# Attention with normalised q and k, followed by an MLP, on one core: order of the first loads, a held reduction, and transposes in another PSUM bank

## The chip, the core and the metric

The kernel runs on one core of a Trainium2 chip. A core has TensorE (PE), which multiplies matrices out of SBUF into the eight banks of PSUM; VectorE (DVE), ScalarE (ACT) and GpSimd (POOL) for elementwise work; and SyncE (SP), which here only issues transfers. SP, ACT and POOL each have a DMA queue. Every engine works through its own list of instructions in order and waits for others by semaphores. The metric is the device time of one execution in microseconds (us); a lower time is better.

## What is computed

```python
q, k, v: (8, 12, 448, 64)      # batch, heads, rows, head size
q_n = q / sqrt(mean(q*q) + 1e-6) * g_q          # over the last axis, k_n likewise with g_k
attn = softmax(q_n @ k_n.T / 8)
x = (attn @ v), laid out as (3584, 768)
h = x @ w_in                                    # 768 x 2048
out = (h * clip(h + 3, 0, 6) / 6) @ w_out       # 2048 x 768
```

The softmax is taken without subtracting the maximum, since q and k are normalised. The sum of a row's exponentials comes out of the product with v, which has a column of ones added.

## The kernel before

Two heads of one batch element make a *pair*: 6 pairs for each of the 8 elements, 48 in all. A pair goes through these steps, each a function of the kernel:

- `loads` (L295): k and q of the pair into one of five `qk` buffers (L302), v into one of five `vf` buffers (L306). For the first three pairs q is issued on ACT's queue, all else on SP's.
- `prep` (L310): squares `sq` (L320 on ACT, L322 on DVE or POOL, L329 on POOL), row sums `ssq` (L337, DVE), reciprocal roots `rs` (L343 and L344, ACT), the scaled copies `qks` in bf16 (L351, DVE or POOL), and v in bf16, `va` (L359, POOL).
- `turn` (L366): k and q are transposed, so that the head size lies along the partitions. For the first ten pairs (P < NPE) PE does it by eight small matmuls against an identity into a PSUM bank (L377), and DVE copies the result out as `kp` (multiplied by gp, the product of both g times 8, L381) and `kq` (L383). Later pairs use transposing DMAs (L388) and multiply kp on DVE or POOL (L392).
- `attend` (L402): scores into two double banks S (L416, PE), exponentials `e` (L421, ACT).
- `gather` (L429): e times v into the bank X, the last 64 rows into the bank R (L437, PE), the reciprocal of the sums and the product `xn` (L462, L463, DVE; for R L502, L503). In the first batch element PE transposes xn through a bank M (L476) and DVE copies it to `xT` (L480); later a DMA does it (L486).

The MLP of a batch element runs while the attention of the next one does: `h_group` computes a column block of h into a bank M (L533, PE), then `t` (L539, ACT) and `gT` (L541, DVE); `y_group` multiplies with w_out (L558, PE), copies (L566, DVE) and stores (L585). The first h groups come with pair 6, the first y groups with pair 10. PSUM holds S 2 x 2 banks, X 1, R 1 and M 2.

The weights come in eight slices over POOL's queue (L277, L283), the first of them after q of pair 2 has landed: POOL copies one element of it into `mark` (L621) before it issues them.

The order of all this is not written out. Each step is given to a planner (`Plan`, L34) with an engine or a choice of engines, an assumed duration, a due time, what it depends on, and `after`, a time in the planner's own clock before which it isn't taken. `begin[P]` is the planned start of pair P; the first pairs are planned 4.1 us apart. The planner runs through its own clock and always takes the step that can start first on any engine (among those of one engine the earliest due), and steps with `lock=True` on DVE and POOL are planned never to overlap. The list sorted by planned start is then written out, so each engine's order is fixed. `after` and due times exist only in planning: on the chip nothing waits for a clock. Each ring of buffers (`Ring`, L129) hands out its buffers in turn, and a step that takes one depends on the last users of the buffer. Only one step on X can thus be under way: a pair's product is normalised out of it before anything else is written to it.

A second order comes from the framework under the kernel. The transfers of SP's and ACT's queues take eight completion semaphores in turn, in the program's order over both queues, and a transfer is only issued when the one eight places before it has landed.

Of the kernel before, what the change touches and what calls it, by code (L numbers as in the profile page):

```python
# [10 lines left out]
MULT = mybir.AluOpType.mult  # L11
ADD = mybir.AluOpType.add
# [4 lines left out]
AX_X = mybir.AxisListType.X  # L17
# [16 lines left out]
class Plan:  # L34
# [12 lines left out]
    def add(self, on, dur, due, fn, *deps, xfer=0.0, after=0.0, lock=False, late=0.0):  # L47
        on, f = ({on: dur}, lambda e: fn()) if isinstance(on, str) else (on, fn)
        s = Step(on, due, f, deps, xfer, after, lock, late, len(self.steps))
        self.steps.append(s)  # L50
        return s
# [93 lines left out]
def kernel(  # L145
# [15 lines left out]
    NJ = H // 2  # L161
# [14 lines left out]
    def tiles(name, n, shape, dt=BF16, pool=const):  # L176
        return [pool.tile(shape, dt, name=f"{name}{i}") for i in range(n)]

    gq_t, gk_t, gp = (const.tile([128, 1], FP32, name=n) for n in ("gq_t", "gk_t", "gp"))
# [23 lines left out]
    X_r = Ring(tiles("X", 1, [128, 512], FP32, psum))  # L203
    R_r = Ring(tiles("R", 1, [128, 512], FP32, psum))
    M_r = Ring(tiles("M", 2, [128, 512], FP32, psum))

    plan = Plan()
    add = plan.add
# [54 lines left out]
    def make_ones():  # L263
# [2 lines left out]
        for t in kp_r.bufs:  # L266
            nc.gpsimd.memset(t[:, S:S + 16], 0.0)

    g_load = add("ACT", 2.2, 0, load_g, after=1.5, late=3.0)
    g_make = add("DVE", 0.1, 0, lambda: nc.vector.scalar_tensor_tensor(  # L270
        out=gp[:], in0=gq_t[:], scalar=8.0, in1=gk_t[:], op0=MULT, op1=MULT), g_load, after=7.5)
    id_make = add("POOL", 0.5, 0, make_ident)
    one_make = add("POOL", 0.6, 0, make_ones)

# [16 lines left out]
    def heads(src, P):  # L291
        b, j = divmod(P, NJ)
        return src[b, 2 * j:2 * j + 2, :, :].rearrange("h (p t) d -> p h (t d)", t=T)

    def loads(P):  # L295
        at = begin[P]
        qk, war, use = qk_r.take()
        res = []
        cost = 0.62 if P < 3 else 0.85
        for i, src in enumerate((k, q)):  # L300
            e = "ACT" if i and P < 3 else "SP"
            res.append(add(e, 0.47, at - 26, lambda i=i, src=src, e=e: {"ACT": nc.scalar, "SP": nc.sync}[e].dma_start(  # L302
                out=qk[0:PT, i], in_=heads(src, P)), *war, xfer=cost, after=max(0.7, at - 24)))
        L[P] = (qk, use, res)
        vf, war, use = vf_r.take()
        s = add("SP", 0.47, at - 19, lambda: nc.sync.dma_start(  # L306
            out=vf[0:PT], in_=heads(v, P)), *war, xfer=cost, after=max(0.7, at - 20))
        V[P] = (vf, use, s)

    def prep(P):  # L310
        at = begin[P]
        hurry = HURRY if P < NJ else 1.0
        qk, qk_use, ld = L.pop(P)
        sq, war, use = sq_r.take()
        engines = {"ACT": nc.scalar, "DVE": nc.vector, "POOL": nc.gpsimd}

        def square(e, i):
            o, x = sq[0:PT, i], qk[0:PT, i]
            if e == "ACT":
                nc.scalar.square(out=o, in_=x)  # L320
            else:
                engines[e].tensor_tensor(out=o, in0=x, in1=x, op=MULT)  # L322

        halves = P < 2 * NJ
        if halves:
            on = {"ACT": 0.63} if P < 3 else {"DVE": 0.68, "POOL": 1.04}
            parts = [add(on, 0, at - 9 * hurry, lambda e, i=i: square(e, i), ld[i], *war, lock=True, after=at - 13) for i in range(2)]
        else:
            parts = [add("POOL", 1.93, at - 10, lambda: nc.gpsimd.tensor_tensor(  # L329
                out=sq[0:PT], in0=qk[0:PT], in1=qk[0:PT], op=MULT), *ld, *war, lock=True, after=at - 14)]  # L330
        ssq, war, ssq_use = ssq_r.take()
        rs, rwar, rs_use = rs_r.take()
        qks, qwar, qks_use = qks_r.take()
        sc = []
        for i0, i1 in ([(0, 1), (1, 2)] if P == 0 else [(0, 2)]):
            cs, n = slice(i0 * 2 * T, i1 * 2 * T), i1 - i0
            red = add("DVE", 0.6 * n, at - 8 * hurry + 0.5 * i0, lambda i0=i0, i1=i1, cs=cs: nc.vector.tensor_reduce(  # L337
                out=ssq[0:PT, cs], in_=sq[0:PT, i0:i1].rearrange("p i h (t d) -> p (i h t) d", d=D),
                axis=AX_X, op=ADD), *(parts[i0:i1] if halves else parts), *war)
            use.append(red)  # L340

            def rstd(cs=cs):
                nc.scalar.activation(out=rs[0:PT, cs], in_=ssq[0:PT, cs], func=LN, bias=D * 1e-6)  # L343
                nc.scalar.activation(out=rs[0:PT, cs], in_=rs[0:PT, cs], func=EXP, scale=-0.5)  # L344

            r = add("ACT", 0.45, at - 7 * hurry + 0.5 * i0, rstd, red, *rwar)
            ssq_use.append(r)
            rs4 = rs[0:PT].rearrange("p (i h t) -> p i h t", i=2, h=2)
            for i in range(i0, i1):
                on = {"DVE": 0.69} if P < 2 and i == 0 else {"DVE": 0.69, "POOL": 1.05} if halves else {"POOL": 1.05}  # L350
                sc.append(add(on, 0, at - 6 * hurry, lambda e, i=i, rs4=rs4: engines[e].tensor_tensor(  # L351
                    out=qks[0:PT, i].rearrange("p t h d -> p h t d"),
                    in0=qk[0:PT, i].rearrange("p h (t d) -> p h t d", d=D),
                    in1=rs4[:, i].unsqueeze(3).to_broadcast([PT, 2, T, D]), op=MULT), r, *qwar, lock=True))
        qk_use += parts + sc
        rs_use += sc
        vf, vf_use, vl = V.pop(P)
        va, war, va_use = va_r.take()
        vc = add({"POOL": 0.61}, 0, at - 3, lambda e: engines[e].tensor_copy(  # L359
            out=va[0:PT, :, :, 0:D], in_=vf[0:PT].rearrange("p h (t d) -> p h t d", d=D)), vl, one_make, *war,  # L360
            lock=True)
        vf_use.append(vc)
        SC[P] = (qks, qks_use, sc, va, va_use, vc)

    def turn(P):
        at = begin[P]  # L366
        qks, qks_use, sc, va, va_use, vc = SC.pop(P)
        kq, war, kq_use = kq_r.take()
        kp, kwar, kp_use = kp_r.take()
        if P < NPE:  # L370
            m, mwar, m_use = M_r.take()
            pt = m[:].bitcast(BF16)[:, 0:2 * S].rearrange("p (i c) -> p i c", i=2)
            tr = []
            for i in range(2):
                def trans(i=i):
                    for t in range(T):
                        nc.tensor.transpose(  # L377
                            out=pt[:, i, t * PT:(t + 1) * PT],
                            in_=qks[0:PT, i, t].rearrange("p h d -> p (h d)"), identity=ident[0:PT, 0:PT])
                tr.append(add("PE", 0.4, at - 2, trans, sc[i], id_make, *mwar))  # L380
            ks = add("DVE", 0.45, at - 1, lambda: nc.vector.tensor_scalar_mul(  # L381
                kp[:, 0:S], pt[:, 0], gp[:, 0:1]), tr[0], g_make, one_make, *kwar)
            qc = add("DVE", 0.45, at - 1, lambda: nc.vector.tensor_copy(out=kq[:, 1], in_=pt[:, 1]), tr[1], *war)  # L383
            m_use += [ks, qc]
            qks_use += tr
            KQ[P] = (kq, kp, va, kq_use, kp_use, va_use, [ks, qc], vc)
        else:
            tr = add("SP", 1.3, at - 8, lambda: nc.sync.dma_start_transpose(  # L388
                out=kq[:].rearrange("p i (t c) -> p (i t) c", c=PT),
                in_=qks[0:PT].rearrange("p i t h d -> p (i t h d)")), *sc, *war, xfer=1.3, late=1.5)  # L390
            ks = add({"DVE": 0.34, "POOL": 0.6}, 0, at - 1, lambda e: (
                nc.vector if e == "DVE" else nc.gpsimd).tensor_scalar_mul(  # L392
                    kp[:, 0:S], kq[:, 0], gp[:, 0:1]), tr, g_make, one_make, *kwar, lock=True)
            qks_use.append(tr)
            kq_use.append(ks)
            KQ[P] = (kq, kp, va, kq_use, kp_use, va_use, [ks], vc)
# [232 lines left out]
    for P in range(NP):  # L629
        for fn, at in ((loads, -26), (prep, -13), (turn, -2), (attend, 0)):  # L630
            blocks.append((begin[P] + at, lambda fn=fn, P=P: fn(P)))
        blocks.append((begin[P + 1] + 0.1, lambda P=P: gather(P)))
# [41 lines left out]
```

## Time and profile before

| what | us |
|---|---|
| median of 8 runs | 442.39 |
| lowest and highest of them | 440.12, 443.93 |
| the profiled execution's own time | 442.73 |
| its span, first to last instruction | 441.0 |
| PE busy | 411.2 (93% of the span) |
| ACT, DVE, POOL busy | 248.9, 246.1, 240.8 |

In the profile each engine's instructions stand with their line in the kernel, and "PEld" is PE's loading of weights, which overlaps its matmuls. The span cut into 40 slices of 11 us shows how the shares change (each digit is the busy share of a slice in tenths, 9 being 90% or more):

```
PE   0588789999999999999999999999999999999996
DVE  0998867657766765456565466456564444334421
ACT  2688478647774676457673667457673665123200
POOL 3499898774856757655775666846767510000000
```

PE has nothing to do in the first slice and is short of work in the next five; from then on it is full. DVE and POOL are fullest in just those early slices. The durations used below come from the one profiled execution.

### The profile page before, as it was taken

Reading aid. Unit: us, or ns where it says so; the run is one execution under the profiler, and the core shown is the slowest. Engines: PE = TensorE matmul, PEld = TensorE weight load, DVE = VectorE, ACT = ScalarE, POOL = GpSimd, SP = SyncE. Lnnn points to the kernel's source line nnn. Section 1 sums busy time; section 2 is a strip of 40 time slices with the busy share of each in tenths; the row PEclk is TensorE's granted clock in tenths of the full one; section 3 lists DMA queues with packets and bytes.
Section 4 is the critical chain, followed back from the end, with each engine's and each line's share of the span. In section 5 each row is a group of like instructions: output and inputs, shape, how many; then the busy total and the mean of one; then the engine's idle time right before and its main releaser. Section 6 shows DMA issues by size and latency. Waiting matters only on the chain.

```text
span 441.0 us, 9205 instructions
## 1 busy us (share of the span) xinstructions
PE 411.2 (93%) x3663; PEld 229.2 (52%) x3682; DVE 246.1 (56%) x417; ACT 248.9 (56%) x425; POOL 240.8 (55%) x230
## 2 busy tenths in 40 slices
PE   0588789999999999999999999999999999999996
PEld 0255445555455555554455555554456555654563
DVE  0998867657766465456565466456564444334421
ACT  2688478647774676457673667457673665123200
POOL 3499898774856757665775666846767510000000
PEclk9999899999999999999999999999999999999999
DMA  9999999978365646675466555684466320420122
GB/s 224 254 267 263 224 216 193 192 174 225 78 149 150 170 120 162 148 209 131 106 165 173 155 147 153 156 208 124 105 163 176 91 60 12 59 77 0 37 71 73
DMA packets 102923, 64.58 MB, mean 146 GB/s; under 512 B 59744, under 2 KB 99424, under 8 KB 102880
## 3 DMA queue, kind: packets, MB, share of 16 engines
q1 hardware_dynamic: 94544, 57.01, 51.6%
q0 software_dynamic: 7296, 6.29, 8.9%
q10 hardware_dynamic: 1040, 0.69, 0.6%
q8 instruction: 29, 0.48, 0.5%
q14 instruction: 14, 0.11, 0.1%
HBM read 45.61 MB, written 11.01 MB: 128 GB/s over the span
## 4 chain that ended last, share of the span: by engine, by line
PE 82%; DVE 6%; ACT 4%; DMA 3%; POOL 3%; issue 2%; SPq 0%; POOLq 0%
PE M L558 27%; PE M L533 26%; PE S L416 8%; PE X L437 8%; PE S L558 4%; PE S L533 2%; PE R L437 2%; DVE ssq L337 2%; ACT e L421 2%; DVE qks L351 1%; PE X L558 1%; DMA gq_t<-in_g_q_dram 1%; POOL qks L351 1%; DVE sq L322 1%; POOL sq L329 1%
## 5 line engine op out<-in xcount | busy, mean ns | idle before, releaser
L421 ACT ACTIVATE e<-S 112x896 bf16<-112x896 f32 x192 | 166.3, 914 | 65.0 <-PE S L416 65.0
L533 PE MATMUL M<-xT,w_in_sb 128*128 128x384 bf16 (+1 forms) x679 | 146.1, 351 | 4.0 <-DVE gT L541 3.2
L351 POOL TENSOR_TENSOR qks<-qk,rs 112x512 bf16<-112x512 f32 x87 | 91.0, 1061 | 89.5 <-ACT rs L344 89.4
L558 PE MATMUL M<-w_out_sb,gT 128*128 128x384 bf16 x736 | 131.8, 326 | 0.0
L558 PEld LDWEIGHTS <-gT 128*128 128x128 bf16 x896 | 82.9, 98 | 57.9 <-issue 7.8
L533 PEld LDWEIGHTS <-w_in_sb 128*128 128x128 bf16 x768 | 69.9, 98 | 68.6 <-issue 14.1
L541 DVE SCALAR_TENSOR_TENSOR gT<-t,M 128x384 bf16<-128x384 f32 (+1 forms) x116 | 70.8, 612 | 60.0 <-ACT t L539 59.3
L539 ACT ACTIVATE t<-M 128x384 f32<-128x384 f32 (+1 forms) x116 | 62.7, 540 | 68.7 <-PE M L533 65.2
L437 PEld LDWEIGHTS <-e 112*128 112x128 bf16 x1536 | 64.9, 99 | 31.4 <-issue 16.0
L337 DVE TENSOR_REDUCE ssq<-sq 112x16 f32<-112x1024 f32 (+1 forms) x49 | 58.4, 1193 | 24.0 <-POOL sq L329 11.3
L329 POOL TENSOR_TENSOR sq<-qk 112x1024 f32<-112x1024 f32 x36 | 68.2, 1893 | 0.0
L416 PE MATMUL S<-kq,kp 64*128 64x448 bf16 x384 | 56.7, 364 | 4.2 <-DVE kp L381 1.7
L437 PE MATMUL X<-va,e 112*128 112x65 bf16 x1152 | 58.4, 195 | 0.8 <-ACT e L421 0.6
L566 DVE COPY y<-M 128x384 f32<-128x384 f32 x46 | 25.6, 556 | 58.5 <-PE M L558 58.3
L359 POOL CAST va<-vf 112x512 bf16<-112x512 f32 x48 | 31.7, 661 | 7.7 <-DMA vf<-in_v_dram 7.4
L392 POOL TENSOR_SCALAR kp<-kq,gp 128x448 bf16<-128x448 bf16 x23 | 32.3, 1405 | 5.9 <-DMA kq<-qks 5.9
L463 DVE TENSOR_TENSOR xn<-X,rd 128x384 bf16<-128x384 f32 x48 | 26.8, 558 | 1.6
L416 PEld LDWEIGHTS <-kp 64*128 64x128 bf16 x384 | 12.3, 94 | 27.9 <-issue 19.3
L377 PE MATMUL M<-ident,qks 112*128 112x112 bf16 x80 | 7.8, 238 | 14.2 <-DVE qks L351 13.6
L437 PE MATMUL R<-va,e 112*128 112x65 bf16 x384 | 20.4, 195 | 0.0
L558 PE MATMUL S<-w_out_sb,gT 128*128 128x384 bf16 x112 | 19.5, 326 | 0.0
L462 DVE RECIPROCAL rd<-X 128x6 f32<-128x6 f32 x48 | 9.2, 192 | 15.8 <-PE X L437 15.7
(42 smaller groups left out, 155.7 us busy)
## 6 DMA issues: line engine op xcount, KB each, us to landing
qk<-in_k_dram SPq DMA_DIRECT2D x48, 224.0 KB, 3.4
vf<-in_v_dram SPq DMA_DIRECT2D x48, 224.0 KB, 3.8
qk<-in_q_dram SPq DMA_DIRECT2D x45, 224.0 KB, 3.8
w_in_sb<-in_moe_w_in_dram POOLq DMA_DIRECT2D x4, 768.0 KB, 10.8
w_out_sb<-in_moe_w_out_dram POOLq DMA_DIRECT2D x4, 768.0 KB, 9.4
out_dram<-y SPq DMA_DIRECT2D x8, 336.0 KB, 3.4
out_dram<-y SPq DMA_DIRECT2D x8, 288.0 KB, 3.3
out_dram<-y SPq DMA_DIRECT2D x8, 240.0 KB, 3.2
```

The lines of the kernel that those rows point to most:

```text
L329: parts = [add("POOL", 1.93, at - 10, lambda: nc.gpsimd.tensor_tensor(out=sq[0:PT], in0=qk[0:PT], in1=qk[0:PT], op=MULT), *ld, *war, lock= ...
L337: red = add("DVE", 0.6 * n, at - 8 * hurry + 0.5 * i0, lambda i0=i0, i1=i1, cs=cs: nc.vector.tensor_reduce(out=ssq[0:PT, cs], in_=sq[0:PT, ...
L351: sc.append(add(on, 0, at - 6 * hurry, lambda e, i=i, rs4=rs4: engines[e].tensor_tensor(out=qks[0:PT, i].rearrange("p t h d -> p h t d"), ...
L359: vc = add({"POOL": 0.61}, 0, at - 3, lambda e: engines[e].tensor_copy(out=va[0:PT, :, :, 0:D], in_=vf[0:PT].rearrange("p h (t d) -> p h t ...
L392: nc.vector if e == "DVE" else nc.gpsimd).tensor_scalar_mul(
L416: nc.tensor.matmul(out=ps[:, a, 0:S], lhsT=kp[rows, c0:c0 + 128], rhs=kq[rows, 1, :], start=True, stop=True)
L421: x = add("ACT", 0.93, at + step * (t0 + i) / T + 0.2, lambda t=t0 + i, ps=ps: nc.scalar.activation(out=e[0:PT, t], in_=ps[0:PT, :, 0:S], ...
L437: nc.tensor.matmul(out=dst[:, a * E1:(a + 1) * E1], lhsT=e[0:PT, t, a, c0:c0 + 128], rhs=va[0:PT, a, t, :], start=(first and a == 0 and t ...
L533: nc.tensor.matmul(out=m[:, 0:n], lhsT=w_in_sb[:, kt, f * 128:(f + 1) * 128], rhs=X[:, kt, :], start=(kt == 0), stop=(kt == NKT - 1))
L539: r = add("ACT", 0.08 + n / 1200, due + span, lambda: nc.scalar.activation(out=t[:, 0:n], in_=m[:, 0:n], func=RELU, bias=0.5, scale=1.0 / ...
L541: g = add("DVE", 0.12 + n / 960, due + span, lambda: nc.vector.scalar_tensor_tensor(out=G[:, f, :], in0=t[:, 0:n], scalar=1.0, in1=m[:, 0: ...
L558: nc.tensor.matmul(out=m[:, 0:HALF], lhsT=G[:, f, i * 128:(i + 1) * 128], rhs=w_out_sb[:, f, cols], start=(f == 0), stop=(f == NFT - 1))
```

## The change

Four edits. The loads of g get an earlier planned time and a due time ahead of all else, so they come first on ACT's queue, and gp may be made from 5.0 on in the planner's clock instead of 7.5. The first pair's q goes to SP's queue. The row sums of pairs 1 and 2 get a time before which the planner doesn't take them (4.6 us before the pair's planned start). And the PE transposes of pairs 6 to 9 (NJ is 6) take the X bank instead of an M bank.

```diff
-    g_load = add("ACT", 2.2, 0, load_g, after=1.5, late=3.0)
+    g_load = add("ACT", 1.95, -99, load_g, after=0.7, late=1.0)
     g_make = add("DVE", 0.1, 0, lambda: nc.vector.scalar_tensor_tensor(
-        out=gp[:], in0=gq_t[:], scalar=8.0, in1=gk_t[:], op0=MULT, op1=MULT), g_load, after=7.5)
+        out=gp[:], in0=gq_t[:], scalar=8.0, in1=gk_t[:], op0=MULT, op1=MULT), g_load, after=5.0)
...
-            e = "ACT" if i and P < 3 else "SP"
+            e = "ACT" if i and 0 < P < 3 else "SP"
...
-                axis=AX_X, op=ADD), *(parts[i0:i1] if halves else parts), *war)
+                axis=AX_X, op=ADD), *(parts[i0:i1] if halves else parts), *war,
+                after=at - 4.6 if 0 < P < 3 else 0.0)
...
-            m, mwar, m_use = M_r.take()
+            m, mwar, m_use = (M_r if P < NJ else X_r).take()
```

Since the planner works on all steps together, these edits also change where other steps stand and, for squares and `qks`, which of DVE and POOL does them. The number of matmuls, of transfers and of exponentials stays the same.

## The prediction

> **What bounds the kernel now.** I read the table of windows first (columns: stretch, its length, then busy us of PE, PE weight load, DVE, ACT, POOL, granted clock, DMA share, GB/s), cut at the first transpose, at the first score matmul of pair 6 and at the first product with w_out:
>
> ```profile
> 0.00:12.10 12.10, 0.00 (x0) 0.00 (x0) 1.97 (x3) 4.00 (x9) 3.35 (x18) 1.00 0.94 220
> 12.10:42.70 30.60, 23.55 (x295) 14.31 (x295) 28.24 (x49) 24.27 (x41) 24.34 (x26) 1.00 1.16 261
> 42.70:76.90 34.20, 29.91 (x311) 16.95 (x307) 26.19 (x47) 24.04 (x47) 30.80 (x30) 0.95 1.17 216
> 76.90:441.00 364.10, 357.77 (x3063) 197.94 (x3080) 189.70 (x320) 196.62 (x330) 182.28 (x158) 1.00 0.51 128
> ```
>
> From 76.9 us on PE is busy 98% of the time: the end is wherever PE stands at 76.9 plus a fixed amount of matmuls. The change can only pay ahead of that point. There PE does nothing for 12.1 us; then DVE is full (28.24 of 30.60); then PE loses 4.29 us of 34.20 while POOL is the fullest (30.80), and the granted clock of 0.95 costs another 1.7.
>
> Second, the timeline of ScalarE and its DMA queue at the start (start, length, instruction, and in brackets the idle time before it):
>
> ```profile
> 4.19 0.53 ACTq L254 DMA_DIRECT2D gq_t<-in_g_q_dram  x1
> 4.75 0.60 ACTq L255 DMA_DIRECT2D gk_t<-in_g_k_dram  x1
> 7.36 0.47 ACTq L254 DMA_DIRECT2D gq_t<-in_g_q_dram  x1
> 8.80 0.47 ACTq L255 DMA_DIRECT2D gk_t<-in_g_k_dram  x1
> 9.32 1.67 ACT L320 ACTIVATE sq<-qk 112x512 f32<-112x512 f32 x3 [7.32 <-DMA gq_t<-in_g_q_dram]
> ```
>
> The four loads of g are not issued back to back, and the squares stand behind them. The built program says why: the loads of SP's and ACT's queues take eight completion semaphores in turn, and a load waits until the one eight before it has landed. g is number 8, 10, 11 and 13 of that order, so it waits for k0, q0, v0 and k2. The last is issued at 8.80; k0 had been in SBUF since 4.17.
>
> Third, the timeline of DVE for pair 0 and the start of pair 1:
>
> ```profile
> 12.64 0.16 DVE L270 SCALAR_TENSOR_TENSOR gp<-gq_t,gk_t 128x1 f32<-128x1 f32 x1 [0.59 <-DMA gk_t<-in_g_k_dram]
> 12.72 0.69 DVE L351 TENSOR_TENSOR qks<-qk,rs 112x512 bf16<-112x512 f32 x1
> 13.32 1.22 DVE L337 TENSOR_REDUCE ssq<-sq 112x16 f32<-112x1024 f32 x1
> 14.45 0.44 DVE L381 TENSOR_SCALAR kp<-M,gp 128x448 bf16<-128x448 bf16 x1
> 14.81 0.38 DVE L383 COPY kq<-M 128x448 bf16<-128x448 bf16 x1
> ```
>
> Pair 0 waits 0.59 us for g, and then pair 1's row sums (1.22) stand in front of pair 0's kp.
>
> Last, PE's waits between 42.7 and 76.9:
>
> ```profile
> PE M L533 <- DVE gT L541: 2.6, 2, 1.6
> PE M L476 <- DVE xn L463: 1.5, 1, 1.5
> ```
>
> 2.6 us go to PE waiting for one of the two M banks, which the MLP shares with the transposes of pairs 6 to 9.
>
> **What the Trainium skill says.** "DMA: Bandwidth & Descriptors", section "Issuing engines are not separate DMA queues": loads issued by different engines run on the same DMA engines, and moving one saves only issue time. The trace agrees: the first eight loads land between 4.17 and about 9.7 us, one per 0.8 us, whichever queue issued them. So the gain must come from what waits on a queue, not from faster loads. "SBUF — State Buffer", section "Who interferes with whom": a DVE instruction with two SBUF inputs and a GpSimd instruction that reads SBUF block each other, and a tensor_reduce does not. The trace agrees: a square on DVE (L322) takes 2.56 us at 17.14 beside POOL's work and 0.69 at 35.90, while ssq stays at 1.2. "TensorE: Matmul & The Clock Gate", Part 1: PE starts at half clock and falls back after idling. Here twelve h matmuls take 3.13 us at 46.74, soon after a gap of 1.5, and 2.12 at 54.84.
>
> **The change, part by part.**
>
> *g first, q0 on SP.* New order of loads: k0, q0 (SP), gq (ACT), k1 (SP), gk, gq (ACT), v0 (SP), gk (ACT): these eight wait for nothing. Then k2 waits for k0, q1 (ACT) for q0, v1 for a g, q2 (ACT) for k1. ACT must issue q1 and q2 before its first square, so the square now waits for k1's landing and q2's issue. k1 landed at about 5.7 before (the load that waits for it went out at 5.71). It keeps third place in the data, so I take 5.45 (5.0 to 6.0) plus 0.5 for the issue: first square at 5.95 instead of 9.32. That is 3.4 us earlier (2.8 to 4.0). Cost: k2, v1 and q2 go out at 4 to 6 instead of at 0.8 to 3, and DMA has a gap of under a microsecond. q2 lands at about 9 to 9.7 instead of 7.9; it opens the weight loads (before at 8.64), now about 1 us later. Hidden: the first w_in product came at 46.74, and four slices take 11 us each. The square of q2 is due at 9.6, so ACT does not wait long for it.
>
> *Row sums of pair 1 behind kq, gp early.* From first square to first score: before 15.25 - 9.32 = 5.93. After, with the same rows: k's sums end at 1.3, gp 0.16, q's sums at 2.1, two qks to 3.5, transposes of q to 4.1, kq to 4.5, score at 4.65. So 1.3 us less, and the first score stands at 10.6 instead of 15.25, 4.65 earlier. But pair 1 pays: ssq 1.22, two squares of k3 and q3 (which DVE now does alone), two qks and ssq of pair 2 all stand ahead of pair 1's kp. Its first exponential comes at about 18.1 against 21.00, so only 2.9 of the 4.65 is left.
>
> *What the planner does with it.* The order of instructions shows what the diff does not: up to pair 6's kq DVE now does 11 squares and qks instead of 8 (3 x 0.69 = 2.1), and eight row sums instead of seven (1.22), because pairs 7 and 8 are prepared earlier. Adding DVE's rows from pair 1's row sums to pair 6's kq: before 26.1 us of work (kp and kq of pair 0 among it), which took 13.32 to 42.37 = 29.05, 90%. After: 26.1 + 2.1 + 1.2 - 0.8 = 28.6 us, from 10.55 on. At 91% (fewer POOL squares and qks beside it) that is 31.4, so kq at 41.95 and pair 6's first score at 42.1 against 42.75. Of 4.65 us, 4.0 is given back to DVE; 0.65 stays (0 to 2.5, by an efficiency of 91 to 97%). The work is not lost: 3.3 us of DVE work for pairs 7 and 8 is done ahead.
>
> *Transposes of pairs 6 to 9 in X.* No operation is added: 8 transposes, kp and kq as before, X for M. There is one X bank. A turn now waits until the pair two before has been normalised out of X (0.2 + 0.56 on DVE), and the next product with v waits for kp and kq. In PE's new order a score that needs the same kp and kq stands ahead of each such product, and two h groups or two scores stand ahead of most transposes, so the wait is covered as long as DVE is prompt. Not covered is pair 6: its transposes wait for an xn behind one qks, two squares and a ssq on DVE (inside the 31.4 above). h groups now alternate cleanly between the two M banks, with scores or products between every two. Following PE, ACT and DVE by rows from 42.1 on, I find idle stretches of 1.15 (xn of pair 5), 0.35 (M bank behind two exponentials) and about 0.5: 2.0 instead of 4.29, so 2.3 us gained (0 to 3.5). The clock loss I leave at 1.7, since a gap of over a microsecond still precedes the first h group. The first w_out product then comes near 74.0 instead of 76.9.
>
> *After that* the orders nearly agree (the same alternation, single neighbours swapped): PE's 6.3 us of idle in 364 stay, as does the tail of 4.4 us after the last matmul at 436.6. At nothing, since only PE's place at 76.9 passes through.
>
> **Sum.** 0.65 + 2.3 = 2.95 us. The profiled execution took 442.73 (span 441.0, 1.7 around it): 442.73 - 2.95 = 439.8. It lay 0.34 above the median of the runs (442.39), so I forecast 439.5 for the median, with an own range of 437.8 to 441.1.
>
> **Rivals.**
> - *The start passes through whole*: DVE runs at 97%, because squares and qks collide less with POOL, and the M waits go. 2.5 + 3.5 = 6.0 gives 436.4. For: four DVE rows were stretched by some 3.8 us together. Against: POOL still casts v and squares beside DVE. Chance 0.18.
> - *DVE takes it all*: pair 6 starts where it did, and the M waits turn into waits for X and xn. 0 to 1.3 gained, 442.0. For: DVE is already at 92% there and gets more. Chance 0.20.
> - *The single X bank serialises pairs 6 to 9* (slower): if DVE comes late to the normalisation, transpose, kp, kq and product run one after another: per pair norm 0.76, transposes 0.56 and a row sum of 1.22 in front = 2.5 of bare PE time. It decides from about two such pairs: 5.0, less the 2.3 no longer gained and the 0.65 kept, is 2 us slower, 444.4. Against: a score that needs the same kp stands in between. Chance 0.13.
> - Forecast: 0.49.
>
> Faster by over 0.3% (1.3 us, about what this measurement can tell from no change): the first rival 0.18 and most of the forecast, 0.46, so 0.64. Within: 0.20 and 0.03, less 0.01 of stray: 0.22. Slower: 0.14. Range for 8 in 10: 435.8 to 443.8; half of the slow case and a little of the fast one are left out.
>
> **What would show it.** g issued from 0.8 us without gaps and the first square near 6 us; first score near 10.6; exponentials of pair 1 near 18; pair 6's score at 41 to 42.5; no wait of L533 for gT over 0.5 us; first w_out near 74. Wrong if the first square waits for q1 or q2 beyond 7.5, if DVE between 12 and 42 shows idle stretches for POOL or loads, or if PE waits on X behind DVE's norm.

## The result and the profile after

The changed kernel takes 446.57 us, median of 11 runs (444.30 to 447.95), against 442.4 for the kernel before on the same chip: ratio 1.010, 95% interval 1.0082 to 1.0117. It is 1% slower, about 4 us, and lies outside the forecast range. The profiled execution took 447.56. Runs more than 1.5% above the fastest of the same kernel (one of the kernel before, two each of e4 and e11 below) are left out of every comparison.

The table of windows of the changed kernel, cut at the same events as before (first transpose, pair 6's first score, first product with w_out; columns as in the prediction):

```profile
0.00:9.70 9.70, 0.00 (x1) 0.01 (x1) 2.10 (x5) 3.97 (x9) 1.62 (x15) 1.00 0.63 189
9.70:48.99 39.29, 28.42 (x288) 17.29 (x289) 33.76 (x52) 25.10 (x43) 26.30 (x30) 0.85 1.17 261
48.99:82.20 33.21, 31.77 (x316) 18.16 (x316) 26.82 (x47) 24.02 (x45) 24.02 (x24) 0.87 0.95 173
82.20:445.80 363.60, 357.97 (x3065) 197.72 (x3080) 187.68 (x321) 196.90 (x330) 181.72 (x158) 1.00 0.50 129
```

The last row is what it was (363.6 against 364.1 us). The first is shorter by 2.4 us, the third by 1.0. All that is lost, and more, is lost in the second: 39.29 us where the kernel before needed 30.60, with DVE busy 5.5 us longer (33.76 against 28.24) and the granted clock of PE at 0.85 instead of 1.00. In the third row PE's idle time is down from 4.29 to 1.44, which is lower than forecast, but its clock is 0.87 instead of 0.95.

The clock column has a gap at the start, in the prediction's table too: the clock's record begins only when PE first comes to full speed, and the column counts the time before as 1.00. The same two score products (448 columns each) tell the real pace (timelines of PE, before, then changed):

```profile
23.38 0.55 PE L416 MATMUL S<-kq,kp 64*128 64x448 bf16 x2
25.64 0.36 PE L416 MATMUL S<-kq,kp 64*128 64x448 bf16 x2 [0.19 <-DVE kq L383]
```

```profile
25.73 0.56 PE L417 MATMUL S<-kq,kp 64*128 64x448 bf16 x2
27.13 0.36 PE L417 MATMUL S<-kq,kp 64*128 64x448 bf16 x2
```

So PE runs at the slow pace from its first product to about 24.9 us before and to about 26.8 after. A granted clock of 1.00 or 0.85 in the second row describes only what comes behind that point.

The start did nearly what it should. ScalarE and its queue in the changed kernel (timeline):

```profile
2.62 0.62 ACTq L255 DMA_DIRECT2D gk_t<-in_g_k_dram  x1
4.30 2.56 ACTq L302 DMA_DIRECT2D qk<-in_q_dram  x2
6.91 1.67 ACT L320 ACTIVATE sq<-qk 112x512 f32<-112x512 f32 x3 [4.90 <-DMA qk<-in_k_dram]
```

The fourth g goes out at 2.62 instead of 8.80 and the first square runs at 6.91 instead of 9.32. The first score follows at 11.81 (15.25 before). Pair 1's first exponential is at 18.7 (21.0), pair 2's at 23.3 (26.0): up to here the changed kernel is 2.3 to 2.7 us ahead. Pair 3's is at 31.3, where the kernel before had 29.8. Between these two pairs 4.2 us are lost. DVE in that stretch (timeline of the changed kernel):

```profile
26.10 3.58 DVE L352 TENSOR_TENSOR qks<-qk,rs 112x512 bf16<-112x512 f32 x1
29.60 0.44 DVE L382 TENSOR_SCALAR kp<-M,gp 128x448 bf16<-128x448 bf16 x1
29.96 0.34 DVE L481 COPY xT<-M 128x384 bf16<-128x384 bf16 x1
30.23 0.37 DVE L384 COPY kq<-M 128x448 bf16<-128x448 bf16 x1
```

and POOL beside it:

```profile
25.53 1.06 POOL L352 TENSOR_TENSOR qks<-qk,rs 112x512 bf16<-112x512 f32 x1
26.53 1.04 POOL L322 TENSOR_TENSOR sq<-qk 112x512 f32<-112x512 f32 x1
27.52 0.61 POOL L360 CAST va<-vf 112x512 bf16<-112x512 f32 x1
28.09 1.03 POOL L322 TENSOR_TENSOR sq<-qk 112x512 f32<-112x512 f32 x1
```

One qks, which takes 0.69 us elsewhere (in the prediction's lines, for one), takes 3.58: POOL runs four operations without a gap, and DVE's ends half a microsecond after the last of them. It belongs to pair 4 and nobody needs it yet, but pair 3's kp and kq stand behind it on DVE. So PE waits. Its waits between the first score and pair 6 (us in total, times, longest):

```profile
PE S L417 <- DVE kq L384: 4.0, 4, 3.2
PE X L378 <- DVE xn L464: 2.3, 1, 2.3
```

In the kernel before, PE's waits for kp and kq between the first transpose and pair 6 were shorter:

```profile
PE S L416 <- DVE kp L381: 1.7, 1, 1.7
PE S L416 <- DVE kq L383: 1.4, 2, 1.2
```

After the two long waits PE's clock is halved, from 30.2 to 40.4 and from 47.3 to 57.5. In the kernel before, once it had come to full speed, it was halved for 3.4 us only. With the start counted, PE is at half clock for about 38 of the changed kernel's first 82 us and for about 16 of the first 77 us before. The second wait is pair 6's first transpose in the X bank, at 46.94. On DVE it is the same picture (changed kernel):

```profile
41.95 3.11 DVE L322 TENSOR_TENSOR sq<-qk 112x512 f32<-112x512 f32 x2
44.99 1.21 DVE L337 TENSOR_REDUCE ssq<-sq 112x16 f32<-112x1024 f32 x1
46.12 0.18 DVE L463 RECIPROCAL rd<-X 128x6 f32<-128x6 f32 x1
46.33 0.56 DVE L464 TENSOR_TENSOR xn<-X,rd 128x384 bf16<-128x384 f32 x1
```

The two squares, of pairs 7 and 8, take 3.11 where two take 1.29 unhindered (in e7 below), and the normalisation out of X waits behind them. From pair 1's row sums to pair 6's kq these stretched squares and qks add 0.4, 1.3, 2.9, 0.2 and 1.8 = 6.6 us to DVE; in the kernel before it was 3.8; the longest stretched row there is

```profile
17.14 2.56 DVE L322 TENSOR_TENSOR sq<-qk 112x512 f32<-112x512 f32 x1
```

That made the theory for the experiments, "the hold": a square or qks of VectorE is held while GpSimd runs its own operations back to back, what stands behind it on VectorE is late, PE waits and its clock drops. Rivals: the single X bank, or the held row sums, cost the time by themselves; or the gain of the start can't reach the end whatever is done.

### The profile page after: what moved, and what is told of

Its sections match the earlier page's. It is cut to its first block, busy times and chain, and to the rows that moved or that the text cites. A ratio compares the mean times of both kernels' runs of the same rounds, so it can differ in the third digit from the quotient of the medians.

```text
span 445.8 us, 9211 instructions
## 1 busy us (share of the span) xinstructions
PE 418.2 (94%) x3665; PEld 233.2 (52%) x3682; DVE 250.4 (56%) x422; ACT 250.0 (56%) x425; POOL 233.7 (52%) x225
## 4 chain that ended last, share of the span: by engine, by line
PE 87%; DVE 7%; issue 1%; POOL 1%; ACT 1%; DMA 1%; SPq 0%; ACTq 0%; POOLq 0%
PE M L534 28%; PE M L559 27%; PE S L417 10%; PE X L438 9%; PE S L559 4%; PE R L438 3%; PE S L534 2%; DVE qks L352 2%; DVE ssq L337 2%; PE X L559 1%; DMA qk<-in_k_dram 1%; DVE sq L322 1%; DVE kp L382 1%; PE M L378 1%; PE R L559 1%
## 5 line engine op out<-in xcount | busy, mean ns | idle before, releaser
L352 POOL TENSOR_TENSOR qks<-qk,rs 112x512 bf16<-112x512 f32 x85 | 87.9, 1050 | 90.7 <-ACT rs L345 88.7
L559 PEld LDWEIGHTS <-gT 128*128 128x128 bf16 x896 | 82.8, 98 | 58.1 <-issue 8.1
L438 PEld LDWEIGHTS <-e 112*128 112x128 bf16 x1536 | 67.8, 101 | 33.5 <-issue 18.2
L417 PE MATMUL S<-kq,kp 64*128 64x448 bf16 x384 | 58.6, 377 | 5.9 <-DVE kq L384 4.0
L438 PE MATMUL X<-va,e 112*128 112x65 bf16 x1152 | 60.3, 199 | 0.7 <-ACT e L422 0.7
L360 POOL CAST va<-vf 112x512 bf16<-112x512 f32 x48 | 30.7, 642 | 26.4 <-DMA vf<-in_v_dram 18.6
L393 POOL TENSOR_SCALAR kp<-kq,gp 128x448 bf16<-128x448 bf16 x22 | 30.9, 1405 | 6.6 <-DMA kq<-qks 3.6
L464 DVE TENSOR_TENSOR xn<-X,rd 128x384 bf16<-128x384 f32 x48 | 26.8, 557 | 1.6
L438 PE MATMUL R<-va,e 112*128 112x65 bf16 x384 | 21.5, 199 | 0.3 <-ACT e L422 0.3
L378 PE MATMUL M<-ident,qks 112*128 112x112 bf16 x48 | 6.0, 291 | 11.1 <-DVE qks L352 10.6
```

What stands on the lines that cost most here:

```text
L417: nc.tensor.matmul(out=ps[:, a, 0:S], lhsT=kp[rows, c0:c0 + 128], rhs=kq[rows, 1, :], start=True, stop=True)
L438: nc.tensor.matmul(out=dst[:, a * E1:(a + 1) * E1], lhsT=e[0:PT, t, a, c0:c0 + 128], rhs=va[0:PT, a, t, :], start=(first and a == 0 and t ...
L559: nc.tensor.matmul(out=m[:, 0:HALF], lhsT=G[:, f, i * 128:(i + 1) * 128], rhs=w_out_sb[:, f, cols], start=(f == 0), stop=(f == NFT - 1))
```

## The experiments

All times in the table are from the start of the span; "pair n" is the first exponential of that pair, from one profiled execution each. Such positions can shift by 2 us from one execution to the next without any change of order (e7 and e13 show it below), and the profiled executions of e8 and e11 took 2.9 us less and 3.0 more than the median of their kernel. The ratio is to the kernel before on the same chip.

| run | first square | pair 3 | pair 5 | pair 6 | first w_out | median | ratio, 95% interval |
|---|---|---|---|---|---|---|---|
| before | 9.3 | 29.8 | 38.4 | 43.2 | 76.9 | 442.4 | 1 |
| changed | 6.9 | 31.3 | 42.2 | 49.6 | 82.2 | 446.57 | 1.0100 (1.0082 to 1.0117) |
| loads only (e1) | 6.6 | 29.1 | 37.0 | 41.8 | 75.6 | 442.44 | 1.0017 (0.9999 to 1.0035) |
| X bank only (e2) | 9.4 | 29.5 | 38.2 | 44.9 | 82.1 | 445.68 | 1.0088 (1.0056 to 1.0120) |
| X bank undone (e3) | 6.4 | 31.2 | 41.0 | 45.2 | 82.8 | 449.59 | 1.0168 (1.0132 to 1.0205) |
| sums not held (e4) | 6.1 | 29.3 | 39.0 | 45.8 | 83.1 | 444.54, 448.50 (two runs) | none |
| qks behind kq (e5) | 7.1 | 29.1 | 39.0 | 46.3 | 79.3 | 444.76 | 1.0072 (1.0036 to 1.0108) |
| GpSimd waits once (e6) | 7.1 | 29.5 | 38.4 | 45.5 | 77.8 | 444.38 | 1.0059 (1.0035 to 1.0083) |
| GpSimd waits each time (e7) | 5.8 | 26.6 | 35.9 | 42.4 | 76.0 | 442.57 | 1.0026 (1.0003 to 1.0050) |
| dummy matmuls (e8) | 7.3 | 31.8 | 40.5 | 47.4 | 79.9 | 448.55 | 1.0147 (1.0104 to 1.0190) |
| before, with waits (e9) | 8.9 | 28.0 | 36.9 | 41.8 | 73.7 | 441.01 | 0.9977 (0.9961 to 0.9994) |
| waits, X bank undone (e10) | 6.5 | 26.5 | 36.9 | 41.3 | 76.5 | 448.03 | 1.0147 (1.0091 to 1.0203) |
| waits, sums not held (e11) | 6.0 | 29.6 | 38.0 | 45.1 | 80.2 | 442.83 | 1.0033 (1.0013 to 1.0052) |
| waits, loads only (e12) | 5.9 | 28.5 | 37.7 | 42.4 | 76.0 | 442.36 | 1.0006 (0.9987 to 1.0025) |
| waits and dummies (e13) | 6.0 | 28.6 | 38.5 | 44.2 | 79.2 | 443.85 | 1.0036 (1.0019 to 1.0054) |
| before, waits, g on GpSimd (e14) | 4.3 | 27.4 | 35.7 | 40.5 | 74.4 | 442.22 | 1.0010 (0.9981 to 1.0038) |
| before, g on GpSimd (e15) | 4.3 | 27.9 | 36.6 | 41.3 | 74.3 | 441.37 | 0.9985 (0.9966 to 1.0005) |

### The parts of the change, one at a time

**e1**, the kernel before with its order kept on all engines; only g stands first and the first q is on SP:

```diff
-        for s in plan.order():
+        todo = plan.order()
+        head = [*first_pair, g_load]
+        for s in head + [s for s in todo if s not in head]:
             s.fn(s.eng)
```

> The order of before on PE, DVE and POOL, unchanged; only the four loads of g come first on ACT's queue and the first q goes out on SP's. Theory 1 (the new loads are good, what loses is the order that the planner made around them): first square near 6.9 us as in the changed kernel, and 1.5 to 3 us of the 2.4 us gained there stay at the end: 439.5 to 441. Rival (the later landing of q2, v1 and the weights costs as much as the start gains): 441.5 to 444, with waits of POOL or ACT for loads between 7 and 20 us.

Measured 442.44, no difference that can be told. The first square gains 2.7 us, pair 1's exponential 0.9, the first w_out product 1.3. Much of the start's gain is gone by pair 1, and the trace shows a new wait in the queue that g is moved ahead of (timelines of ScalarE, then of POOL, in e1):

```profile
10.32 1.15 ACT L323 ACTIVATE sq<-qk 112x512 f32<-112x512 f32 x2 [1.28 <-DMA qk<-in_q_dram]
11.66 0.63 ACT L323 ACTIVATE sq<-qk 112x512 f32<-112x512 f32 x1 [0.19 <-DMA qk<-in_q_dram]
```

```profile
11.69 0.18 POOL L624 COPY mark<-qk 1x1 f32<-1x1 f32 x1 [10.08 <-DMA qk<-in_q_dram]
11.82 0.61 POOL L362 CAST va<-vf 112x512 bf16<-112x512 f32 x1
```

The q loads of pairs 1 and 2 stand behind the four g on ScalarE's queue. ScalarE waits for them, and POOL's `mark`, which waits for pair 2's q, comes at 11.69 instead of 7.96, with all of POOL's work behind it.

**e2**, the X bank alone in the kernel before, and **e3**, the changed kernel with that line undone; the line is

```diff
-            m, mwar, m_use = M_r.take()
+            m, mwar, m_use = (M_r if P < NJ else X_r).take()
```

> The kernel before with the transposes of pairs 6 to 9 in the X bank and nothing else; the orders are those of before up to pair 6. Theory 1: the X bank does no harm by itself, PE's waits for M banks between 43 and 62 us (2.6) shrink: 440 to 442.5. Rival (the single X bank serialises pairs 6 to 9): 445 to 447, PE waits for xn ahead of the X transposes.

> The changed kernel with the transposes of pairs 6 to 9 back in the M banks; its orders are those of the changed kernel up to pair 6. Theory 1: the loss lies ahead of pair 6 and stays: 445.5 to 448, pair 3's first score near 30.5 and pair 6's near 48 to 49. Rival (the X bank is the loss): back to 439 to 442.

Both are slower than the kernel before, 445.68 and 449.59. e2 lies where the rival had put it; e3 lies above both of its ranges. So the line is neither the whole loss nor harmless. In e2 PE waits 1.6 us for xn at the entry to pair 6, as the rival had it, but a longer wait follows. In e2 the start and the first pairs are those of the kernel before; then DVE (timeline of e2)

```profile
47.37 4.21 DVE L322 TENSOR_TENSOR sq<-qk 112x512 f32<-112x512 f32 x1
```

holds an xT behind a single square for 4.21 us, and PE waits for that xT 3.09 at 52.50. In e3 the qks at 26.05 takes 3.57 as in the changed kernel: the hold there has nothing to do with the X bank. One effect goes with the X bank throughout the table. From pair 5 to pair 6 it takes 5.7 to 7.4 us in all nine kernels with the X bank (5.7 only in e13, with dummies) and 4.2 to 4.9 in all eight without.

**e4**, the changed kernel without the hold on the row sums:

```diff
-                axis=AX_X, op=ADD), *(parts[i0:i1] if halves else parts), *war,
-                after=at - 4.6 if 0 < P < 3 else 0.0)
+                axis=AX_X, op=ADD), *(parts[i0:i1] if halves else parts), *war)
```

> The changed kernel without the time before which the planner doesn't take the row sums of pairs 1 and 2. Theory 1: another order of DVE and POOL up to pair 6, so another place for the collisions of DVE and POOL; if the held sums brought the bad order, 439 to 442.5, if any replanning with the new loads does, 444 to 448. Rival (held sums are the gain of the change, the rest the loss): slower than the changed kernel, over 447.

Four runs took 444.54, 448.50, 452.96 and 454.14, too far apart for a ratio. All are above the highest run of the kernel before (443.92), so undoing this part does not repair the kernel.

### The hold itself

**e5** moves one step of the changed kernel behind three others on VectorE:

```diff
+        at = {s.n: s for s in todo}          # 84: qks of pair 4; 134: kq of pair 3
+        todo.remove(at[84])
+        todo.insert(todo.index(at[134]) + 1, at[84])
```

> One move in the changed kernel: VectorE's qks of pair 4 stands behind kp, xT and kq of pair 3 instead of ahead of them. Theory (a two-input operation of VectorE is held while GpSimd runs its own operations back to back, and what stands behind it on VectorE waits too): pair 3's first exp falls from 31.3 to 27.5 to 28.5 us and TensorE's wait of 3.16 us for that kq goes; the same hold, up to 3 us, is met by the same qks later, when nothing urgent is behind it; the program gains 1 to 4 us, 442.5 to 445.5. Rival (the single X bank and the queued row sums cost the time, the hold only fills time that was lost anyway): pair 3 earlier, but pair 6's first exp stays at 49 to 50 and the time at 446 to 447.5.

Measured 444.76, pair 3 at 29.1. PE's waits for kq before pair 6 fall from 4.0 us to 1.8. The moved qks now starts at 28.57, beside one last square of POOL's run, and takes 1.56. Pair 6 is at 46.3 instead of 49.6, so the rival (it stays at 49 to 50) is out. The gain in total is not certain, since the interval overlaps that of the changed kernel. The later holds are still there (3.11 at 38.63, 3.34 at 48.77).

**e6** leaves VectorE's order and lets GpSimd wait once, by copying one element of the result of that qks (`probe[84]`) ahead of its own square:

```diff
+            if s.n == 110:                    # GpSimd's square that started at 26.53
+                nc.gpsimd.tensor_copy(out=mark[:], in_=probe[84])
             s.fn(s.eng)
```

> The order of the changed kernel stays on VectorE. GpSimd gets one copy of a single element out of VectorE's qks of pair 4, ahead of its square that starts at 26.53, so that this square can't begin before that qks is done. Theory of the hold: the qks takes 1.2 to 1.7 us instead of 3.58 (it waits for the one GpSimd operation that is under way, then runs its 0.69), pair 3's first exp comes at 29 to 29.5 instead of 31.3, the program gains 0 to 3 us. Rival (the qks is slow for another reason, such as its own data or DMA traffic): the qks still takes over 3 us and GpSimd's square starts late by as much.

This is the direct test. DVE, then POOL, in e6:

```profile
26.97 1.03 DVE L355 TENSOR_TENSOR qks<-qk,rs 112x512 bf16<-112x512 f32 x1
28.05 0.45 DVE L386 TENSOR_SCALAR kp<-M,gp 128x448 bf16<-128x448 bf16 x1
```

```profile
26.39 1.05 POOL L355 TENSOR_TENSOR qks<-qk,rs 112x512 bf16<-112x512 f32 x1
28.14 0.18 POOL L650 CAST mark<-qks 1x1 f32<-1x1 bf16 x1 [0.69 <-DVE qks L355]
28.28 1.03 POOL L323 TENSOR_TENSOR sq<-qk 112x512 f32<-112x512 f32 x1
```

With POOL made to stand aside for 0.69 us, the same qks takes 1.03 instead of 3.58. Its data and its place in VectorE's order are unchanged, so it was POOL's following operations that held it. The program is at 444.38, about 1.8 us less by the ratios, with intervals that just touch.

**e7** does this for every square and qks of VectorE that the planner put ahead of a GpSimd operation, in the first 62 us of the planner's clock:

```diff
+        held = [s for s in todo if s.eng == "DVE" and s.lock and s.n in probe and s.start < 62.0]
         for s in todo:
+            if s.eng == "POOL" and s.lock:
+                due = [d for d in held if d.end <= s.start + 0.001]
+                if due:
+                    nc.gpsimd.tensor_copy(out=mark[:], in_=probe[due[-1].n])
+                    held = [d for d in held if d not in due]
             s.fn(s.eng)
```

> As the run before, but for every square and qks of VectorE that the planner put ahead of a GpSimd operation in the first 62 us: GpSimd copies one element of VectorE's result before it goes on. The order on the other engines stays. Theory: no square or qks of VectorE takes more than 1.8 us, TensorE's waits for kq and xn in the first 78 us fall from over 6 us to under 3, the first w_out product comes at 77 to 80 instead of 82.2, and the program at 440 to 444. If GpSimd's own waits make its squares, qks and va late instead: VectorE's operations are short, but the first w_out product stays at 81 to 84 and the time at 445 to 449.

Measured 442.57: of the 1.0% that the change lost, 0.74% is back. Pair 3 comes at 26.6 and pair 5 at 35.9, 2.5 us ahead of the kernel before. This profiled execution had an early full clock (score products at 0.36 from 20.51 on), so part of that lead is its own. Its windows around pair 6 and the MLP stage:

```profile
9.00:41.80 32.80, 22.77 (x287) 14.34 (x288) 28.80 (x53) 25.08 (x44) 25.81 (x35) 0.98 1.16 255
41.80:76.00 34.20, 32.16 (x315) 18.16 (x314) 24.85 (x47) 24.05 (x45) 25.48 (x30) 0.87 1.22 227
```

DVE's busy time up to pair 6 is 28.8 us, where the changed kernel had 33.8. What is left is in the second row: PE is idle for only 2.04 of 34.20 us, but its clock is 0.87. (The 0.98 in the first row again leaves out the slow start up to 20.)

**e9** is the kernel before with the same copies.

> The kernel before with GpSimd's one-element copies: GpSimd goes on only when a square or qks of VectorE that the planner put ahead of it is done (the first 62 us). Nothing else differs. If the hold is what sets the changed kernel apart, the kernel before has little to gain: its longest hold is 2.56 us at 17.14, for pair 3's square, and the time is 440.5 to 442.5. If GpSimd's overlaps cost the kernel before as much as the changed one: 437 to 439.5, and the change would be worth nothing even without the hold.

441.01, ratio 0.9977: the kernel before gains 1.0 us, the changed one 3.3 (0.74% of 442). It is the fastest of all kernels here by its ratio, and the only one whose interval lies wholly below 1. It also shows that the hold is not all: with the copies in both, the changed kernel is still about 2 us behind (1.0026 against 0.9977).

### What the other two microseconds are

**e8** fills the two long waits of PE in the changed kernel with products that nobody uses; **e13** fills the short ones (0.2 to 0.9 us) of e7 between pair 5 and the first h group:

```diff
+            n, bank = {142: (44, warm["s"][:, 0, 0:128]), 209: (34, warm["m"][:, 0:128])}.get(s.n, (0, None))
+            for _ in range(n):
+                nc.tensor.matmul(out=bank, lhsT=ident[:], rhs=ident[:], start=True, stop=True)
             s.fn(s.eng)
```

> The changed kernel with 44 products of ident with ident (128 columns each, results overwritten) ahead of pair 3's first score and 34 ahead of pair 6's first transpose through the X bank, where TensorE otherwise sits idle for 3.2 and 2.3 us. They compute nothing that is used. If the half clock that follows those two waits costs by itself: no half clock from 30 to 40 and from 47 to 57, pair 6's first exp 1 to 3 us earlier, the program 2 to 4 us faster (442.5 to 444.5). If the pace in this stretch is VectorE's and not TensorE's: full clock, the same times, 446 to 447.5.

> The changed kernel with GpSimd's one-element copies (442.57 without dummies) and 54 short products of ident with ident in the places between pair 5's first score and pair 5's last transpose of xn where TensorE waited 0.2 to 0.9 us. They compute nothing that is used. There the half clock ran from 40.3 to 50.6. If this half clock is what still separates it from the kernel before with copies (441.01): no half clock in 38 to 52, the first w_out product at 73.5 to 75 instead of 76.0, the program at 440 to 441.5. If ScalarE and VectorE set the pace there: full clock, the same 442 to 443.5.

e8's four runs (445.67 to 449.63) show no gain in total, though the half clock from 30 to 40 is gone; whether the added products cost time themselves is not shown. Its profile, the fastest of the four, has a full clock from 29.1 to 49.6, and pair 3 to pair 6 takes 15.6 us against 18.3. In e13 the clock is full from 32.3 to 76.7, and pair 6 to pair 9 takes 22.1 us against 25.1 in e7: in these two executions the half clock costs about 3 us.

Up to its first added product, at 37.3, e13 has e7's order on every engine. Yet in e13's profile PE came to full clock at 32.3 instead of 20.2, and pair 3 at 28.6 instead of 26.6. Pair 1 was already 0.6 us later in e13, so some 1.4 us go with the longer slow start; what sets its length no run shows.

The total does not follow the saved 3 us: 443.85, above both forecasts. A next limit is in the timelines of POOL and PE of e13:

```profile
68.60 1.41 POOL L400 TENSOR_SCALAR kp<-kq,gp 128x448 bf16<-128x448 bf16 x1 [5.49 <-PE R L445]
```

```profile
76.05 1.51 PE L541 MATMUL M<-xT,w_in_sb 128*128 128x384 bf16 x6 [3.75 <-DVE gT L549]
```

This kp is the first whose k and q are transposed by a DMA. The profile names PE as what ended the wait, but this kp uses none of that product; the transposition it needs was issued at 56.64 and landed 11.9 us later, at 68.5. POOL's next square stands behind this kp, DVE waits 4.07 us for that square with a gT behind it, and PE waits 3.75 for the gT. In the kernel before, the first two were issued at 63.24 and 65.92 and took 4.9 to 6.5 us.

**e14** and **e15** start the kernel before earlier in another way: g goes over GpSimd's queue, which is idle there, so that no q stands behind it. e14 has the copies too.

```diff
-            nc.scalar.dma_start(out=gq_t[a * 64:(a + 1) * 64, :], in_=g_q.rearrange("(p o) -> p o", o=1))
-            nc.scalar.dma_start(out=gk_t[a * 64:(a + 1) * 64, :], in_=g_k.rearrange("(p o) -> p o", o=1))
+            nc.gpsimd.dma_start(out=gq_t[a * 64:(a + 1) * 64, :], in_=g_q.rearrange("(p o) -> p o", o=1))
+            nc.gpsimd.dma_start(out=gk_t[a * 64:(a + 1) * 64, :], in_=g_k.rearrange("(p o) -> p o", o=1))
```

> The kernel before with GpSimd's one-element copies (441.01), and the four loads of g issued from GpSimd's queue instead of ScalarE's: the q loads stay where they were, ScalarE's first square has no g ahead of it any more, and GpSimd is idle until 7.96 anyway. If the start passes through when no q load becomes late for it: first square at 5 to 7 instead of 8.9, pair 2's first exp at 21.5 to 23 instead of 24.2, the program at 438 to 440, the fastest so far. If the gain of the start is swallowed before the MLP stage whatever the order: 440.5 to 441.5.

> The kernel before with only the four loads of g moved to GpSimd's queue, without copies. Tells the two parts of the run before apart. If both act by themselves: 439 to 441 (between the 442.0 of before and the run with both). If the start is worth nothing without the copies: 441.5 to 443.

The first square comes at 4.3, five microseconds earlier than before, and in e15 the first w_out product at 74.3 instead of 76.9. The totals, 442.22 and 441.37, can't be told from the kernel before. e14 is ahead of e9 by 1.3 us at pair 6 and behind it by 0.7 at the first w_out. The place is the same DMA transposition (timelines of POOL and of PE in e14):

```profile
69.71 1.41 POOL L396 TENSOR_SCALAR kp<-kq,gp 128x448 bf16<-128x448 bf16 x1 [1.41 <-DMA kq<-qks]
```

```profile
71.17 0.55 PE L420 MATMUL S<-kq,kp 64*128 64x448 bf16 x4 [1.38 <-POOL kp L396]
```

Issued at 58.89 and 61.79, the first two transpositions took 10.7 and 9.2 us to land. PE waits there 1.4 us in e14 and 1.2 in e15; in e9, where they were issued at 59.72 and 62.36 and took 8.5 and 7.0 us, it does not.

**e10, e11, e12**: e3, e4 and e1 with the copies.

> The changed kernel without its last part (pairs 6 to 9 are transposed through the two M banks again), with GpSimd's one-element copies. If the single X bank costs at the entry to pair 6 (6.5 us from pair 5's to pair 6's first exp in the run with copies and X bank, 4.8 in the kernel before): pair 6's first exp at 40 to 41.5 and the time at 439.5 to 441.5. If the X bank helps as forecast (TensorE's waits for M behind gT, 2.6 us in the kernel before): those waits are back, the first w_out product at 76.5 to 78 and the time at 443 to 444.5, above the 442.57 with the X bank.

> The changed kernel without the hold on the row sums of pairs 1 and 2, with GpSimd's one-element copies. If the hold on the sums is worth the 0.6 to 1 us that gp and kp gain at pair 0: pair 0's first exp 0.6 to 1.2 us later than the 12.7 with the hold, later pairs within 0.5 us, time 442 to 444. If the hold on the sums costs more later than it gains at pair 0: pair 2 and after earlier, and 440 to 441.5.

> The order of the kernel before on every engine, only the loads of g first on ScalarE's queue and the first q on SyncE's, with GpSimd's one-element copies. Loads alone gave 442.44, with the first w_out product at 75.6. If the copies help here as in the changed kernel (4 us): 438 to 440, the fastest so far. If there is little hold left to take away in that order: 441.5 to 443.

e12 (442.36, against 442.44 in e1) shows that it is not the hold that keeps e1's start from paying. The late q loads are the likely reason, but that is argued: in e14 and e15 no q is late, and they do not gain in total either. In e11 pair 0's first exponential is at 14.2 against 12.7 in e7, so holding the sums is worth 1.5 us there; the total, 442.83, is the same as e7's. Its later pairs come 1.3 to 3 us after e7's, but in an execution 3.0 us slower than its median. e10 was a miss, 448.03 instead of 439.5 to 444.5. It is level with e7 up to the first w_out product (76.5 against 76.0) and loses 6.5 us after it, in the profiled executions. ScalarE, then PE, in e10:

```profile
81.00 0.22 ACT L347 ACTIVATE rs<-ssq 112x16 f32<-112x16 f32 x1 [4.91 <-DVE ssq L340]
```

```profile
82.31 0.56 PE L421 MATMUL S<-kq,kp 64*128 64x448 bf16 x2 [3.70 <-ACT e L426]
```

The reciprocal roots of a later pair stand on ScalarE ahead of exponentials that PE needs, and wait for a row sum whose square POOL finishes at 79.7. One line less for the X bank lets the planner write another order at pair 11. e3 has that order too and ScalarE's longest such wait there is 2.1 us, so the order alone does not explain e10. So e3 and e10 don't price the X bank alone. The step from pair 5 to pair 6 in the table suggests about 2 us for it; from pair 6 to the first w_out product e7 takes 33.6 us and e10 35.2, so most of that comes back.

## Why the prediction was wrong

- **The start** was right in kind. First square forecast at 5.95, measured 6.91, since k1 landed about 1 us later than assumed (in runs with the same order of first loads the square came at 5.75 to 7.3). From there to the first score 4.65 forecast, 4.90 measured. Pair 1 forecast at 18.1, measured 18.7.
- **"At 91% (fewer POOL squares and qks beside it) that is 31.4, so kq at 41.95"** is the step that failed. From pair 1's row sums to pair 6's kq it took 37.26 us (11.67 to 48.93), so the 28.6 us of work were done at 77%. The added rows were counted rightly (11 squares and qks, eight row sums). But the stretching rose from 3.8 to 6.6 us, and DVE's idle time from 1.6 (29.05 less 27.43 busy) to 4.8 (37.26 less 32.44 busy). Of the 4.8, 4.5 are four waits for PE (1.34, 0.96, 1.09, 1.14), three of them in the half clock from 30.2 to 40.4. The prediction had quoted the cause, a square stretched from 0.69 to 2.56, and then treated it as an efficiency that carries over from one order to another. Which operation is held, for how long, and what stands behind it depends on where POOL's runs fall. The planner's `lock` assumes that these steps don't overlap, but no wait enforces it. With the hold taken out (e7) the same stretch takes 30.3 us, 11.43 to 41.75: kq within 0.2 us of the forecast. That closeness is partly luck of one execution, since in e13 it takes 32.4 us, 11.30 to 43.71, after a longer slow start.
- **The MLP stage.** Forecast: PE's idle time from 4.29 to 2.0. Measured: 1.44, and 2.04 in e7. The wait of h for gT is 0.3 us, as named. **"The clock loss I leave at 1.7"** failed: PE was busy 31.77 us for work that takes 28.2 at full clock (29.91 less the 1.7), so 3.6 were lost, and 4.0 in e7. Ahead of pair 6 the prediction put no further loss of clock, where the changed kernel ran at half clock again from 30.2 to 40.4. With this term e7's first w_out product, forecast at 74.0, lands at 76.0.
- **The sum.** The first w_out product came at 82.2 instead of 74.0: 1.1 by the later start, 5.9 by DVE's stretch, 1.3 by the MLP stage.
- **Afterwards the same** held: 363.6 us.
- **Rivals.** None of the three was what happened. "The single X bank serialises" had the sign and 444.4. (Its sum takes off 2.3 us that it calls no longer gained; without that it gives 446.7, near the measured time, but not for its reason.) Its bank did cost at pair 6 (PE's one wait of 2.3 for xn), but pairs 7 to 9 were not serialised: after pair 6's entry PE waits 0.2 us for the X bank. The largest loss came before any pair used the bank. "The start passes through whole" failed on the hold; where the hold is gone or small, the start still brings no gain in total that can be told (e7, e12 to e15), and the traces point to the clock and the DMA transpositions at pair 10.

What stays open: the last 2 us between the two kernels with copies (e7 and e9), where half clock, X bank and transpositions were seen but no run brought the time back; what sets the length of the slow start; and why the transpositions take so long when they are issued earlier (8.5 to 11.9 us for the first one in e9 and e13 to e15, but 7.3 in e7). The w_out slices are loaded at that time over POOL's queue; no run separated the two.

## What to carry to other kernels

Where two engines hold each other up, an average efficiency doesn't carry over to a new order: list each stretched row, what POOL ran beside it, and which urgent step would stand behind it. If a planner assumes that two engines' steps exclude each other, a wait that makes it so can be cheap: copies of one element (0.18 us each) took 3.3 us out of the changed kernel and 1.0 out of the one before. An earlier start is worth only what the later resources let through; here PE waited for a transfer at pair 10. And where a clock record begins late, check PE's pace by the length of one kind of product.

## What the runs showed of the hardware

- The Trainium skill, "SBUF — State Buffer", section "Who interferes with whom", says that VectorE and GpSimd share a pair of ports under "an exclusive lock" and that a VectorE instruction with two SBUF inputs contends with a GpSimd instruction that reads SBUF. The traces agree and show more: the held VectorE operation also lost to the operations that POOL started later, 0.69 us becoming 3.58 here and 4.21 in e2, until POOL's run ended. Row sums stayed at 1.21 beside the same work.
- The Trainium skill, "TensorE: Matmul & The Clock Gate", Part 1, gives about 3.4 us of sustained work for the way back to full clock. Here the half clock lasted 10.2 us twice in one execution, with PE busy for most of it (9.37 us, then 8.90), and 3.4 us in the kernel before. The measurement decides: waits of 3.2 and 2.3 us were each followed by 10 us at half clock. At the start the half clock lasted 10.7 us from PE's first product in e7 and 23.0 in e13, with the same order.
- The first DMA transposition of a pair's k and q took 6.5 us from issue to landing in the kernel before and 11.9 us in e13.
